# A fused attention and cosine FFN on one core: tile 0 cut in two halves around tile 1, with the start ordered from a list of pieces

## The chip, the cores and the metric

The kernel runs on one core of a Trainium2 chip. The metric is the device time of one execution in microseconds (us). Five engines matter here: TensorE (PE in the profile; its weight loads are listed as PEld), VectorE (DVE), ScalarE (ACT), GpSimd (POOL) and SyncE (SP), which issues the DMAs. Each engine runs its own instructions in a fixed order and waits on semaphores.

## The reference, cut to what matters

```
def reference(q, k, v, w_in, w_out):          # q, k, v: 8 x 8 heads x 576 x 64, float32
    ...                                       # split into 9 chunks of 64 along the sequence
    scores = scale * np.matmul(q_c, k_c.transpose(0, 1, 2, 4, 3))     # 64 x 64 per chunk
    scores = scores - np.max(scores, axis=-1, keepdims=True)
    attn = np.exp(scores)
    attn = attn / (np.sum(attn, axis=-1, keepdims=True) + 1e-09)
    out = np.matmul(attn, v_c)
    x = out.transpose(0, 2, 1, 3).reshape(4608, 512)
    h = x @ w_in                              # 512 x 2048
    g = h * np.cos(h)
    return (g @ w_out).astype(np.float32)     # 2048 x 512
```

The attention is local to chunks of 64 tokens. The two weights come as 8-byte floats; everything else is 4-byte.

## The kernel before, in words

The 4608 tokens are nine tiles (t = 0 to 8) of 512 tokens. d_ff is cut into 16 chunks (fc) of 128. For each tile there is attention, which makes x, and then 16 steps. A step has one `hidden(t, fc)` (L333), which makes h for one chunk of d_ff, one `activate(t, fc, h)` (L347), which makes g = h cos h, and one `project` (L366), which adds g times a chunk of w_out into the four banks acc0 to acc3. Project runs LAG = 3 steps behind hidden.

Precision is kept by splitting each operand of the big products into a high and a low part and multiplying high by high, high by low and low by high: three matmuls in place of one. Hidden is therefore 4 x 3 = 12 matmuls of 128x128 by 512 columns, and project is 12 as well. All of them are recorded on the helper line L74.

*Weights.* `load_weight` (L98) brings each chunk in as 8-byte words, 512 KB for each of w_in and w_out. `split_weight` (L111) makes 4-byte words of them and splits these: on ACT L124, L125 and L126 and the high part at L136; on DVE L127, L130 and the low part at L137. There are 32 such weights (16 w_in, 16 w_out). They are split once, during tile 0, and stay in SBUF for all tiles. The decoded words lie in a buffer `w` with two places and in `half0` and `half1`; later the same buffers carry output to DMA.

*Activation.* ACT makes a whole number of turns from h (L353), DVE subtracts it (L354), ACT takes the sine (L356), DVE multiplies by h (L357), ACT copies the high part (L360) and DVE makes the low part (L361). h lies in one of two PSUM banks, which come free after L357.

*Attention.* `scores_early` (L175) and `scores` (L191) write scores to PSUM; DVE takes the largest of each row and subtracts it; ACT takes the exponential; DVE sums, inverts and multiplies (the quotient); the weights of the values are transposed, on PE for tiles 0 and 1 (`transposed`, L258) and on DVE for later ones (`turned`, L273); `weighted` (L290) multiplies with the values, and ACT and DVE split the result into the high and low parts of x (L321, L322). The score matmuls and those of `weighted` are 64x64; for a later tile they come in four groups of 64 recorded matmuls. In tile 1 the quotient is one instruction on POOL (L232). Exponentials and sines need different tables on ACT, and changing them is a table load.

*What sets the order.* The main loop (L461) runs over s = 16 t + fc, tiles in turn. During tile t the attention of tile t + 1 is done in its steps (`attend`, `attend_early`). From tile 1 on (`ordered`) every PE, ACT and DVE instruction keeps program order, and the pieces of attention stand in three queues (`soon`, `late`, `full`) from which `activate` takes. For tile 0, before that flag is set, the order on each engine is chosen by the framework's own scheduler. `split_weight` is called AHEAD = 2 chunks ahead. DMAs, all on SP, are ordered by that scheduler throughout.

*Buffers.* x of a tile takes four buffers of a pool of eight; two of tile 0's values borrow one of them. The scores `e` of a tile have one buffer. At a tile's last project `finish` (L380) copies each acc bank (two on ACT, L389, two on DVE, L391) and sends it out.

Of the kernel before, what the change touches and what calls it, by code (L numbers as in the profile page):

```python
# [20 lines left out]
P = 128  # L21
# [8 lines left out]
AHEAD = 2  # L30
# [10 lines left out]
def attention_then_cos_ffn(ctx: ExitStack, tc, qT, kT, v, w_in, w_out, out, wide):  # L41
# [24 lines left out]
    ordered = False  # L66

    def kept(ins):
        if ordered:
            tc.keep_in_program_order(ins)  # L70
        return ins
# [39 lines left out]
    def split_weight(name, fc):  # L111

        raw, n = w_raw.pop((name, fc))
        w = dec.tile([P, n], F32, name="w")
        if not wide:
            nc.gpsimd.tensor_copy(w, raw[:, :n])
        else:
            top = raw[:, 4 : 4 + 4 * n].rearrange("p (n k) -> p n k", k=4)[:, :, 0]
            mid = raw.bitcast(U32)[:, 1 : 1 + 2 * n].rearrange("p (n k) -> p n k", k=2)[:, :, 0]


            half, low = half_words[(name == "out")], w.bitcast(U32)
            hb = half[:, :, 1]
            nc.scalar.activation(hb.bitcast(BF16), top.bitcast(BF16), AF.Abs)  # L124
            nc.scalar.activation(hb, hb, AF.Relu, bias=float(7 - (MORE << 7)), scale=8.0)  # L125
            nc.scalar.activation(low, mid, AF.Relu, bias=float((1 << 19) - 1), scale=-(2.0**-13))  # L126
            nc.vector.scalar_tensor_tensor(  # L127
                hb, top, 0x8000, hb, op0=ALU.bitwise_and, op1=ALU.bitwise_or
            )
            nc.vector.tensor_tensor(  # L130
                low, low, half.rearrange("p n k -> p (n k)").bitcast(U32), op=ALU.bitwise_xor
            )
        o = SHIFT if name == "in" else 0
        parts = wts.tile([P, 2 * n + PAD], F32R, name=f"w_{name}{fc}")
        hi, lo = parts[:, o : o + n], parts[:, o + n : o + 2 * n]
        nc.scalar.copy(out=hi, in_=w)  # L136
        nc.vector.tensor_tensor(lo, w, hi.bitcast(F32), op=ALU.subtract)  # L137
        w_parts[name, fc] = (hi, lo)
# [6 lines left out]
    probs = {}  # L145
    def load_qk(t, hp):
        qt, kt = (att.tile([P, TOK], F32, name=n, bufs=HP) for n in ("qt", "kt"))
        nc.sync.dma_start(out=qt, in_=qT[t, hp])
        nc.sync.dma_start(out=kt, in_=kT[t, hp])
        queries[t, hp] = (qt, kt)  # L150

    def load_v(t, hp):

        if t or hp < 2:
            vt = att.tile([P, TOK], F32, name="vt")
        else:
            if hp == 2:
                values["roomy"] = xp.tile([P, 2, TOK], F32, name="x")
            vt = values["roomy"][:, hp - 2]
# [10 lines left out]
    def weights_of(t):  # L170
        if t not in probs:
            probs[t] = att.tile([P, HP, NCH, CH], F32, name="e", bufs=1)
        return probs[t]

    def scores_early(t, hp, s):  # L175

        qt, kt = queries.pop((t, hp))
        for c in range(NCH):
# [5 lines left out]
        e = weights_of(t)  # L184
        m = att.tile([P, NCH], F32, name="m", bufs=4)
        nc.vector.tensor_reduce(out=m, in_=sv, op=ALU.max, axis=AX.X)
        nc.vector.tensor_tensor(
            e[:, hp], sv, m.unsqueeze(2).broadcast_to([P, NCH, CH]), op=ALU.subtract
        )

    def scores(t, g, banks):  # L191
# [14 lines left out]
        e = weights_of(t)[:, 2 * g : 2 * g + 2].rearrange("p a (r h) k -> p a r h k", h=2)  # L206
        for h in range(2):
# [10 lines left out]
            soon.extend((largest, below))  # L218

    def softmax(t, a, b):  # L220

        n = (b - a) * NCH
        e = probs[t][:, a:b].rearrange("p a c k -> p (a c) k")
        nc.scalar.activation(e, e, AF.Exp, scale=SCALE)
        z = att.tile([P, HP * NCH], F32, name="z")
        zs = z[:, :n]
        nc.vector.tensor_reduce(out=zs, in_=e, op=ALU.add, axis=AX.X)
        nc.vector.tensor_scalar(zs, zs, 1e-9, None, op0=ALU.add)
        nc.vector.reciprocal(out=zs, in_=zs)

        eng = nc.gpsimd if t == 1 else nc.vector
        eng.tensor_tensor(e, e, zs.unsqueeze(2).broadcast_to([P, n, CH]), op=ALU.mult)  # L232

    def exponentials(t):
        e = probs[t].rearrange("p a c k -> p (a c k)")
        kept(nc.scalar.activation(e, e, AF.Exp, scale=SCALE))

    def divide(t):

        z = att.tile([P, HP, NCH], F32, name="z")  # L240

        def total(hp):
            kept(nc.vector.tensor_reduce(out=z[:, hp], in_=probs[t][:, hp], op=ALU.add, axis=AX.X))

        def inverse():
            kept(nc.vector.tensor_scalar(z, z, 1e-9, None, op0=ALU.add))
            kept(nc.vector.reciprocal(out=z, in_=z))

        def quotient(hp):
            e = probs[t][:, hp]  # L250
            zb = z[:, hp].unsqueeze(2).broadcast_to([P, NCH, CH])
            kept(nc.vector.tensor_tensor(e, e, zb, op=ALU.mult))

        soon.extend(lambda hp=hp: total(hp) for hp in range(HP))
        soon.append(inverse)
        return [lambda hp=hp: quotient(hp) for hp in range(HP)]

    def transposed(t, hp):  # L258


        e = probs[t][:, hp]
        pts = att.tile([P, TOK], F32, name="pts")
        pt = ps_h.tile([P, 512], F32, name="h") if t == 0 else bank("a", 0)
        for c in range(0, NCH, 2):
            nc.tensor.transpose(
# [3 lines left out]
            )  # L269
        nc.scalar.copy(out=pts, in_=pt)  # L270
        probs[t, hp] = pts

    def turned(t, hp):  # L273
# [3 lines left out]
        src = probs[t][:, hp].rearrange("p c (x k) -> p c x k", k=BL)  # L277
# [12 lines left out]
    def weighted(t, hps, banks):  # L290
# [18 lines left out]
        if (t, g) not in x_parts:  # L309
            x_parts[t, g] = tuple(  # L310
                xp.tile([P, 2, TOK], F32R, name="x") for _ in range(2)
            )
        for par in range(2):
# [6 lines left out]
            def split(xq=xq, hi=hi, lo=lo):  # L320
                kept(nc.scalar.copy(out=hi, in_=xq))  # L321
                kept(nc.vector.tensor_tensor(lo, xq, hi.bitcast(F32), op=ALU.subtract))  # L322

            if t < EARLY:
                split()
            else:
                late.append(split)


    g_parts = {}  # L330
    acc = {}

    def hidden(t, fc):  # L333
        if t == 0 and fc in (2, 3):
            h = bank("a", fc)
        else:
            h = ps_h.tile([P, TOK], F32, name="h")
# [9 lines left out]
    def activate(t, fc, h):  # L347
# [5 lines left out]
        kept(nc.scalar.activation(n, h, AF.Identity, bias=0.25, scale=0.5 / math.pi))  # L353
        kept(nc.vector.scalar_tensor_tensor(g, n, -2.0 * math.pi, h, op0=ALU.mult, op1=ALU.add))  # L354
        take(soon, 1)
        kept(nc.scalar.activation(g, g, AF.Sin, bias=0.5 * math.pi))  # L356
        kept(nc.vector.tensor_tensor(g, h, g, op=ALU.mult))  # L357
        take(soon, 1)
        take(full, 2)
        kept(nc.scalar.copy(out=g_hi, in_=g))  # L360
        kept(nc.vector.tensor_tensor(g_lo, g, g_hi.bitcast(F32), op=ALU.subtract))  # L361
        g_parts[t, fc] = (g_hi, g_lo)
# [3 lines left out]
    def project(t, fc):  # L366
        g_hi, g_lo = g_parts.pop((t, fc))
        w_hi, w_lo = w_parts["out", fc]
        for sub in range(NSUB):
            if fc == 0:  # L370
# [3 lines left out]
            matmul(o, g_hi[:, ss], w_hi, start=(fc == 0), stop=False)  # L374
            matmul(o, g_hi[:, ss], w_lo, start=False, stop=False)
            matmul(o, g_lo[:, ss], w_hi, start=False, stop=(fc == NFC - 1))
            if fc == NFC - 1:
                full.append(lambda sub=sub, o=o: finish(t, sub, o))

    def finish(t, sub, o):  # L380
        if t == NT - 1:
            if sub % 2 == 0:
                acc["last"] = xp.tile([P, 2, DM], F32, name="x")
            os = acc["last"][:, sub % 2]
        else:

            os = (wts if sub % 2 else dec).tile([P, DM], F32, name=f"half{sub // 2}" if sub % 2 else "w")
        if sub % 2 == 0:
# [3 lines left out]
        r0 = t * TOK + sub * P  # L392
        nc.sync.dma_start(out=out[r0 : r0 + P, :], in_=os)


    def attend_early(t, step):
        if step < HP:
            scores_early(t, step, bank("a", step))
        if step == HP - 1:
            softmax(t, 0, HP)  # L400
        hp, odd = divmod(step - HP - 1, 2)
        if 0 <= hp < HP and not odd:
            transposed(t, hp)
            weighted(t, (hp,), (bank("a", 0), bank("a", 1)))
            if hp + 2 < HP:
                load_v(t, hp + 2)
# [3 lines left out]
    def attend(t, step):  # L410

        for g in range(2):
            if step == g:
                scores(t, g, (bank("a", 0), bank("a", 1)))
            if step == 8 + 5 * g:
                weighted(t, (2 * g, 2 * g + 1), (bank("a", 0), bank("a", 1)))
# [3 lines left out]
        if step == 3:  # L420
            pieces["quotients"] = divide(t)

        soon.extend(pieces["quotients"][a] for a in {4: (0, 1), 5: (2,), 6: (3,)}.get(step, ()))
# [12 lines left out]

    for hp in range(HP):
        load_qk(0, hp)
    load_weight("in", 0)
    for hp in range(HP):  # L440
        load_v(0, hp)
    for fc in range(NFC):
        if fc:
            load_weight("in", fc)
# [92 lines left out]
```

## Time and profile before

| | us |
|---|---|
| median of 3 runs (lowest, highest) | 880.68 (880.52, 880.91) |
| the profiled execution | 880.95 |
| its span, first to last instruction | 879.1 |
| PE busy in the span | 853.0 |
| mean granted PE clock | 0.986 |

| stage of the span, us | DMA, GB/s | granted PE clock |
|---|---|---|
| 10 to 20 | 409 | 0.79 |
| 20 to 30 | 401 | 0.50 |
| 30 to 40 | 406 | 0.67 |
| 50 to 60 | 405 | 1.00 |
| 70 to 80 | 0 | 1.00 |
| 200 to 300 | 43 | 1.00 |

A row of the timeline has its start, its duration, the engine, the line, the operation, the tile that it writes and those it reads, the shapes and a count; in brackets is how long the engine was idle before it and what released it. Matmuls are pipelined, so the durations of matmuls that follow each other overlap; the distance of their starts is what one costs. "x" in a count column is a number of instructions. Line numbers are those of the kernel before.

### The profile page before, as it was taken

How to read it: one execution, taken by the hardware profiler on the slowest of the kernel's cores; microseconds unless marked ns; L12 is line 12 of the kernel's file. 1: busy time of each engine (PE TensorE's matmuls, PEld its weight loads, DVE VectorE, ACT ScalarE, POOL GpSimd, SP SyncE). 2: the span in 40 equal slices, each digit the busy share in tenths (PEclk: the TensorE clock that was granted, in tenths of full speed). 3: DMA queues.
4: the chain of work that ended last, by engine and by line, in shares of the span. 5: the costliest groups of instructions: out<-in, count | busy, mean ns of one | idle time of the engine just before them, and what ended most of it. 6: DMA issues, size and time to landing. Idle time of an engine off the chain costs nothing.

```text
span 879.1 us, 14100 instructions
## 1 busy us (share of the span) xinstructions
PE 853.0 (97%) x5792; PEld 697.1 (79%) x5792; DVE 576.7 (66%) x975; ACT 407.9 (46%) x660; POOL 5.5 (1%) x9
## 2 busy tenths in 40 slices
PE   4899999999999999999999999999999999999998
PEld 3587777888888888888888888888888888888886
DVE  5999986766577656764686558655766577644332
ACT  4998993533354335333533344333533354333332
POOL 0001000000000000000000000000000000000000
PEclk8599999999999999999999999999999999999999
DMA  9980013100310012001300040003100010001001
GB/s 346 406 340 33 14 25 110 47 26 25 96 49 25 24 49 96 25 1 50 120 1 25 25 145 1 25 25 97 49 25 25 1 48 25 1 1 48 1 1 48
DMA packets 25407, 55.42 MB, mean 63 GB/s; under 512 B 2816, under 2 KB 2816, under 8 KB 25344
## 3 DMA queue, kind: packets, MB, share of 16 engines
q1 hardware_dynamic: 25344, 54.54, 17.7%
q8 instruction: 45, 0.74, 0.4%
q14 instruction: 18, 0.15, 0.1%
HBM read 45.09 MB, written 9.44 MB: 62 GB/s over the span
## 4 chain that ended last, share of the span: by engine, by line
PE 85%; ACT 11%; DMA 1%; DVE 1%; issue 1%; SPq 0%; ACTq 0%
PE acc L74 41%; PE h L74 40%; PE a L74 4%; ACT half L124 2%; ACT half L125 2%; ACT w L126 2%; DMA w_out<-in_w_out_dram 1%; ACT g_hi L360 1%; ACT g L356 1%; ACT w_out L136 1%; ACT w_in L136 1%; ACT g L353 1%; DMA kt<-in_kT_dram 1%; ACT pts L270 0%; ACT x L321 0%
## 5 line engine op out<-in xcount | busy, mean ns | idle before, releaser
L74 PE MATMUL h<-x,w_in 128*128 128x512 f32 x1704 | 416.9, 393 | 5.9 <-ACT x L321 2.8
L74 PEld LDWEIGHTS h<-x,w_in 128*128 128x128 f32 x1704 | 321.1, 189 | 75.0 <-DVE g L357 4.5
L74 PE MATMUL acc<-w_out,g_hi 128*128 128x512 f32 x1152 | 355.2, 392 | 0.0
L74 PEld LDWEIGHTS acc<-w_out,g_hi 128*128 128x128 f32 x1152 | 214.0, 188 | 45.2
L74 PE MATMUL acc<-w_out,g_lo 128*128 128x512 f32 x576 | 221.1, 390 | 0.6 <-DVE g_lo L361 0.6
L354 DVE SCALAR_TENSOR_TENSOR g<-g,h 128x512 f32<-128x512 int32 x142 | 97.2, 684 | 138.3 <-ACT g L353 137.6
L353 ACT ACTIVATE g<-h 128x512 int32<-128x512 f32 x142 | 84.7, 596 | 190.1 <-PE h L74 190.1
L361 DVE TENSOR_TENSOR g_lo<-g,g_hi 128x512 fp32r<-128x512 f32 x144 | 102.5, 712 | 79.9 <-ACT g_hi L360 77.0
L356 ACT ACTIVATE g<-g 128x512 f32<-128x512 f32 x144 | 91.0, 632 | 128.2 <-DVE g L354 128.0
L360 ACT CAST g_hi<-g 128x512 fp32r<-128x512 f32 x144 | 89.3, 620 | 128.9 <-DVE g L357 79.3
L357 DVE TENSOR_TENSOR g<-h,g 128x512 f32<-128x512 f32 x142 | 98.1, 691 | 56.5 <-ACT g L356 53.0
L74 PEld LDWEIGHTS acc<-w_out,g_lo 128*128 128x128 f32 x576 | 108.1, 188 | 23.7 <-DVE g_lo L361 1.1
L282 DVE STREAM_TRANSPOSE pts<-e 32x256 f32<-32x256 f32 x224 | 97.4, 435 | 3.7
L125 ACT ACTIVATE half<-half 128x512 uint16<-128x512 uint16 x32 | 25.1, 786 | 0.2
L74 PEld LDWEIGHTS a<-kt,qt 64*64 64x64 f32 x1024 | 18.9, 135 | 7.6 <-issue 6.8
L130 DVE TENSOR_TENSOR w<-w,half 128x512 uint32<-128x512 uint32 x32 | 22.0, 687 | 1.8 <-ACT w L126 1.0
L74 PEld LDWEIGHTS a<-pts,vt 64*64 64x64 f32 x1024 | 16.6, 134 | 7.2 <-issue 5.3
L322 DVE TENSOR_TENSOR x<-a,x 128x512 fp32r<-128x512 f32 (+1 forms) x38 | 21.9, 614 | 0.1
L74 PE MATMUL a<-kt,qt 64*64 64x64 f32 x1024 | 21.8, 222 | 0.0
L74 PE MATMUL a<-pts,vt 64*64 64x64 f32 x1024 | 19.0, 222 | 0.7 <-ACT pts L270 0.7
L216 DVE TENSOR_TENSOR e<-a,m 128x512 f32<-128x512 f32 x28 | 19.2, 686 | 0.5
L212 DVE TENSOR_REDUCE m<-a 128x8 f32<-128x512 f32 x28 | 19.2, 684 | 0.0
(61 smaller groups left out, 316.5 us busy)
## 6 DMA issues: line engine op xcount, KB each, us to landing
qt<-in_qT_dram SPq DMA_DIRECT2D x36, 256.0 KB, 4.0
kt<-in_kT_dram SPq DMA_DIRECT2D x36, 256.0 KB, 4.2
vt<-in_v_dram SPq DMA_DIRECT2D x34, 256.0 KB, 3.0
w_in<-in_w_in_dram SPq DMA_DIRECT2D x16, 512.0 KB, 9.1
w_out<-in_w_out_dram SPq DMA_DIRECT2D x16, 512.0 KB, 9.4
out_dram<-w SPq DMA_DIRECT2D x16, 256.0 KB, 2.1
out_dram<-half SPq DMA_DIRECT2D x16, 256.0 KB, 2.0
out_dram<-x SPq DMA_DIRECT2D x4, 256.0 KB, 2.0
```

Of the source, the lines that this page charges most:

```text
L74: kept(nc.tensor.matmul(*args, **kw))
L125: nc.scalar.activation(hb, hb, AF.Relu, bias=float(7 - (MORE << 7)), scale=8.0)
L130: nc.vector.tensor_tensor(low, low, half.rearrange("p n k -> p (n k)").bitcast(U32), op=ALU.bitwise_xor)
L212: kept(nc.vector.tensor_reduce(out=m, in_=sv, op=ALU.max, axis=AX.X))
L282: kept(nc.vector.transpose(out=dst[o : o + BL, :, qb], in_=src[i : i + BL, :, kb]))
L322: kept(nc.vector.tensor_tensor(lo, xq, hi.bitcast(F32), op=ALU.subtract))
L353: kept(nc.scalar.activation(n, h, AF.Identity, bias=0.25, scale=0.5 / math.pi))
L354: kept(nc.vector.scalar_tensor_tensor(g, n, -2.0 * math.pi, h, op0=ALU.mult, op1=ALU.add))
L356: kept(nc.scalar.activation(g, g, AF.Sin, bias=0.5 * math.pi))
L357: kept(nc.vector.tensor_tensor(g, h, g, op=ALU.mult))
L360: kept(nc.scalar.copy(out=g_hi, in_=g))
L361: kept(nc.vector.tensor_tensor(g_lo, g, g_hi.bitcast(F32), op=ALU.subtract))
```

## The change

Tile 0's steps are cut in two: fc 0 to 7 (GROUP = 8) come first, then all 16 steps of tile 1, then fc 8 to 15 of tile 0, then tiles 2 to 8. The sums of tile 0's first half are copied from the acc banks to SBUF, written to a tensor in HBM (`partial`), read back after tile 1's last project (`resume`), and added on DVE when tile 0's second half is done. The second half of the weights is due only from step 16 on.

The instructions of these first 32 steps, with the splitting of all weights and the attention of tiles 0, 1 and 2, are no longer issued as the program comes to them. Each becomes a piece: engine, length, a function that issues it, the pieces that it follows, an earliest time (estimated arrival of a load), and a lag. The pieces get due times backward from the big PE pieces, which are taken to start at WAIT = 23 and to follow each other without a gap; then a list rule picks, for the engine that can start soonest, the piece due earliest among those that can start within 0.2 us of the soonest. The functions are called in that order, and every instruction of PE, ACT, DVE and POOL keeps it (`kept` always holds).

The rest follows from these: in tiles 0 and 1 the exponentials are taken per head pair, and all eight of them before the first sine (`raised`); tile 0's first two quotients and tile 1's four are single POOL instructions of 128x512, where tile 1 had one of 128x2048; tile 1's `weighted` takes two head pairs at a time; `e` is two buffers, e0 and e1; x has two sets of four buffers, x0 for tile 0, x1 for tiles 1 and 2, and then in turn; hidden always uses the two h banks; the loads of tile 1's queries and keys come ahead of the weights, and w_out's two chunks behind w_in's.

The diff, cut to its core:

```
-AHEAD = 2
+GROUP = 8
...
-    xp = ctx.enter_context(tc.tile_pool(name="xp", bufs=8))
+    xp = ctx.enter_context(tc.tile_pool(name="xp", bufs=4))
+    hbm = ctx.enter_context(tc.tile_pool(name="hbm", bufs=1, space=bass.MemoryType.DRAM))
...
     def kept(ins):
-        if ordered:
-            tc.keep_in_program_order(ins)
+        tc.keep_in_program_order(ins)
...
+    def x_room(t, dtype):
+        return xp.tile([P, 2, TOK], dtype, name=f"x{(t + (t > 1)) % 2}")
...
+    order = [(0, fc) for fc in range(GROUP)] + [(1, fc) for fc in range(NFC)]
+    order += [(t, fc) for t in range(NT) if t != 1 for fc in range(0 if t else GROUP, NFC)]
+    partial = [hbm.tile([P, DM], F32, name=f"partial{sub}") for sub in range(NSUB)]
...
+    def finish(t, sub, o, whole):
+        if not whole:
+            os, to = att.tile([P, DM], F32, name="vt" if sub % 2 else "pts"), partial[sub]
+        elif t == 0:
+            os = acc["partial", sub]
...
+        if whole and t == 0:
+            kept(nc.vector.tensor_tensor(os, os, o, op=ALU.add))
...
+    def resume():
+        for sub in range(NSUB):
+            os = acc["partial", sub] = out_room(sub)
+            nc.sync.dma_start(out=os, in_=partial[sub])
...
+    def piece(eng, length, run, *after, at=0.0, lag=0.15):
+        work.append([eng, length, run, [a for a in after if a is not None], at, length + lag])
+        return len(work) - 1
...
+    STAGE = 2 * NFC
+    for fc in range(NFC):
+        s = fc if fc < GROUP else GROUP + fc
+        due["in", fc], due["out", fc] = s, s + LAG
...
+        a = piece(ACT, 0.65, rest_of(key, 0), xored.get(name), at=here[name, fc])
+        r = piece(ACT, 0.65, rest_of(key, 1), a)
+        m = piece(ACT, 0.52, rest_of(key, 2), two_back, at=here[name, fc])
+        g = piece(DVE, 0.63, rest_of(key, 3), r)
+        xored[name] = piece(DVE, 0.6, rest_of(key, 4), m, g)
+        h = piece(ACT, 0.52, rest_of(key, 5), xored[name])
+        split[name, fc] = piece(DVE, 0.6, rest_of(key, 6), h)
...
+                if t or hp < 2:
+                    q[hp] = piece(POOL, 1.0, lambda hp=hp: quotient(t, hp, nc.gpsimd), i)
+                else:
+                    q[hp] = piece(DVE, 0.6, lambda hp=hp: quotient(t, hp), i)
...
+            if t and hp == 1:
+                def values_next():
+                    for j in (2, 3):
+                        load_v(t, j)
+                piece(SP, 0.1, values_next, now)
...
+        stream = piece(
+            PE, 2.72, made_by(key, hidden, t, fc), stream, split["in", fc], bank_at,
+            *x_done[t], *([turned_out[0, 1]] if s < 2 else ()),
+        )
...
+        for i, (eng, length) in enumerate(((DVE, 0.6), (ACT, 0.55), (DVE, 0.6), (ACT, 0.53), (DVE, 0.6)), 1):
+            a = piece(eng, length, rest_of(key, i), a, *([projected.get(s - LAG)] if i == 4 else raised if i == 2 else ()))
...
+    WAIT = 23.0
+    clock = WAIT
+    for i, w in enumerate(work):
+        if w[0] == PE and w[1] > 2:
+            due_at[i] = clock
+            clock += w[1]
+    for i in x_done[2]:
+        due_at[i] = clock - 8.0
+    for i in reversed(range(len(work))):
+        for a in work[i][3]:
+            due_at[a] = min(due_at[a], due_at[i] - work[a][5])
...
+                near = [
+                    (d if e != PE or work[i][1] > 2 else 0.0, start, i)
+                    for start, d, i in c if start <= soonest + 0.2
+                ]
...
+    for start, i in sorted(starts):
+        work[i][2]()
...
-    for s in range(NT * NFC + LAG):
+    for s in range(STAGE, len(order) + LAG):
```

More of the change, by code (lines that the diff above doesn't have):

```diff
@@ L127, in split_weight @@
[L127 to L136, printed above, removed]
@@ L234, in exponentials @@
[L234 to L256, printed above, removed]
+            found.extend((largest, below))
@@ new lines, in scores, with exponentials, total @@
+        return found
+    def exponentials(t, *hps):
+        for e in [weights_of(t, hp // 2)[:, hp % 2] for hp in hps] or [weights_of(t, g) for g in range(2)]:
+            e = e.rearrange("p c k -> p (c k)" if hps else "p a c k -> p (a c k)")
+            kept(nc.scalar.activation(e, e, AF.Exp, scale=SCALE))
+    sums = {}
+    def total(t, hp):
+        if hp == 0:
+            sums[t] = att.tile([P, HP, NCH], F32, name="z")
+        kept(nc.vector.tensor_reduce(out=sums[t][:, hp], in_=weights_of(t, hp // 2)[:, hp % 2], op=ALU.add, axis=AX.X))
@@ L420, in attend @@
         if step == 3:
-            pieces["quotients"] = divide(t)
-        soon.extend(pieces["quotients"][a] for a in {4: (0, 1), 5: (2,), 6: (3,)}.get(step, ()))
+            soon.extend(lambda hp=hp: total(t, hp) for hp in range(HP))
+            soon.append(lambda: inverse(t))
+        for hp in {4: (0, 1), 5: (2,), 6: (3,)}.get(step, ()):
+            soon.append(lambda hp=hp: quotient(t, hp))
         if 4 <= step < 8 or 9 <= step < 13:
@@ new lines, in attention_then_cos_ffn, with made_by, go, rest_of @@
+    made = {}
+    def made_by(key, run, *args):
+        def go():
+            made[key] = run(*args)
+        return go
+    def rest_of(key, i):
+        return lambda: made[key][i]()
+    STAGE = 2 * NFC
+    segment = {x: s for s, x in reversed(list(enumerate(order)))}
+    due = {}
+    for fc in range(NFC):
+        s = fc if fc < GROUP else GROUP + fc
+        due["in", fc], due["out", fc] = s, s + LAG
+    split = {}
+    xored = {}
+    turn_of = sorted(due, key=lambda b: (due[b], b))
@@ new lines, in attention_then_cos_ffn @@
+    WAIT = 23.0
+    clock = WAIT
+    due_at = [1e9] * len(work)
+    for i, w in enumerate(work):
[7 more added lines that the diff above has]
+            due_at[a] = min(due_at[a], due_at[i] - work[a][5])
+    free_at = [0.0] * 5
+    ends = {}
+    starts = []
+    todo = set(range(len(work)))
+    while todo:
+        best = None
+        can = [[] for _ in range(5)]
+        for i in todo:
+            if all(a in ends for a in work[i][3]):
+                e = work[i][0]
+                start = max([free_at[e], work[i][4]] + [ends[a] for a in work[i][3]])
+                can[e].append((start, due_at[i], i))
+        for e, c in enumerate(can):
+            if c:
+                soonest = min(c)[0]
+                near = [
+                    (d if e != PE or work[i][1] > 2 else 0.0, start, i)
+                    for start, d, i in c if start <= soonest + 0.2
+                ]
+                d, start, i = min(near)
+                if best is None or start < best[0]:
+                    best = (start, i)
+        start, i = best
+        todo.remove(i)
+        starts.append((start, i))
+        free_at[work[i][0]] = start + work[i][1]
+        ends[i] = start + work[i][5]
```

411 lines of the change are left out of this document (292 added, 119 removed).

## The prediction

> **What bounds the kernel now.** I read the page's totals first, then busy time by stage, then TensorE (PE) in order of time, then the chain of waits for ScalarE (ACT) and the timeline of VectorE (DVE).
>
> ```profile
> span 879.1 us, 14100 instructions
> PE 853.0 (97%) x5792; PEld 697.1 (79%) x5792; DVE 576.7 (66%) x975; ACT 407.9 (46%) x660; POOL 5.5 (1%) x9
> ```
>
> A share of 97% seems to leave PE nothing to gain. It is a mean, and busy time also counts matmuls that run at a lower clock. The stages say more (columns: stretch, its length, then busy time and instructions of PE, PEld, DVE, ACT, POOL; granted clock, DMA share, GB/s; the borders are explained below):
>
> ```profile
> 6.35:20.00 13.65, 6.75 (x136) 6.04 (x136) 11.55 (x22) 7.36 (x13) 0.00 (x0) 0.85 1.03 398
> 20.00:69.49 49.49, 43.47 (x364) 33.42 (x357) 45.74 (x81) 49.14 (x89) 0.00 (x0) 0.80 0.93 362
> 69.49:140.70 71.21, 65.90 (x461) 51.50 (x460) 62.76 (x98) 62.16 (x111) 3.89 (x1) 1.00 0.09 25
> ```
>
> From 20 to 69.49 us ACT is busy 49.14 of 49.49 us and DVE 45.74: the weights are decoded and split there, beside tile 0's steps. To see what PE has to show for it I count in units: a unit is 12 matmuls of 512 columns, one hidden or one project. Matmuls that read w_in, then those that read w_out, in the first 69.49 us and after 140.70 us; then two steps of the last tile, and a step with a group of 64 attention matmuls:
>
> ```profile
> 0.00:69.49 69.49, 22.39 (x72) 0.83 0.93 356
> 0.00:69.49 69.49, 11.33 (x48) 0.83 0.93 356
> 140.70:879.10 738.40, 366.02 (x1524) 1.00 0.12 39
> 140.70:879.10 738.40, 378.15 (x1561) 1.00 0.12 39
> ...
> 780.20 2.88 PE L74 MATMUL h<-x,w_in 128*128 128x512 f32 x12
> 785.64 2.88 PE L74 MATMUL h<-x,w_in 128*128 128x512 f32 x12
> ...
> 226.28 2.88 PE L74 MATMUL h<-x,w_in 128*128 128x512 f32 x12
> 229.10 1.16 PE L74 MATMUL a<-kt,qt 64*64 64x64 f32 x64
> 233.04 2.88 PE L74 MATMUL h<-x,w_in 128*128 128x512 f32 x12
> ...
> 875.18 0.39 PE L74 MATMUL acc<-w_out,g_lo 128*128 128x512 f32 x1
> ```
>
> A step (two units) takes 785.64 - 780.20 = 5.44 us, so a unit takes 2.72. A step with an attention group takes 233.04 - 226.28 = 6.76, so the group costs 1.32. After 140.70 us there are (1524 + 1561)/12 = 257 units and 27 groups (four for each of tiles 2 to 8, one of them done): 140.7 + 257 x 2.72 (699.0) + 27 x 1.32 (35.6) = 875.3, and the last matmul ends at 875.57. So nothing is lost after 140.7; there the kernel is PE at full rate. All loss lies before. By 69.49 us PE has done (72 + 48)/12 = 10 units, worth 27.2 us; from there to 140.70 it does 21 units, 57.1 us of work in 71.2, beside tile 1's attention. The change touches this start and must be judged there.
>
> **The yardstick.** Call T8 the time at which tile 1's first hidden (step 8 of the new order) can start. Before it PE must have done 8 hidden and 5 projects: 13 units. Attention of tile 1, w_in 0 to 7 and w_out 0 to 4 must be done: 13 weights. Afterwards 275 units (748.0) and 28 groups (37.0) are left, then the tail of 879.1 - 875.57 = 3.5, and the profiled execution's own time of 880.95 is 1.85 above its span. It lies 0.27 above the median 880.68, which I neglect.
>
> **ACT up to T8.** Pieces of its chain of waits (start, length to the next piece, what), and one with the table load:
>
> ```profile
> 91.87 0.51 ACT w_in L136
> 92.38 0.69 ACT half L124
> 93.07 0.42 ACT pts L270
> 93.49 0.56 ACT w L126
> 94.05 0.68 ACT half L125
> 94.73 0.46 ACT g_hi L360
> 95.19 0.49 ACT g L353
> 97.47 0.47 ACT g L356
> 99.77 0.21 ACT x L321
> ...
> 79.12 1.28 ACT L356
> ```
>
> A weight is 0.51 + 0.69 + 0.56 + 0.68 = 2.44; 13 of them 31.7. A step's activation is 0.49 + 0.47 + 0.46 = 1.42; five whole ones and two without the last copy (which their banks don't need) are 9.0. Eight exponentials at 0.47, taken like the sine of that size, 3.8; eight copies of transposes at 0.42, 3.4; x copies of tile 0 eight at 0.21 and of tile 1 four at 0.46, 3.5; one table load 1.3. Sum 52.7.
>
> ```profile
> 6.35 0.69 DVE L186 TENSOR_REDUCE m<-acc 128x8 f32<-128x512 f32 x1 [6.35 <-PE acc L74]
> 7.80 0.63 ACT L224 ACTIVATE e<-e 128x512 f32<-128x512 f32 x1 [5.79 <-DVE e L187]
> ```
>
> ACT starts at 7.80 and loses 12.2 - 7.36 = 4.8 by 20 us waiting for data, and 0.35 after; the loads at the front don't get faster. 7.8 + 52.7 + 5.2 = 65.7.
>
> **DVE up to T8.** Starts of instructions that follow each other:
>
> ```profile
> 61.05 0.70 DVE L357 TENSOR_TENSOR g<-a,g 128x512 f32<-128x512 f32 x1
> 61.65 0.70 DVE L130 TENSOR_TENSOR w<-w,half 128x512 uint32<-128x512 uint32 x1
> ...
> 63.66 0.75 DVE L127 SCALAR_TENSOR_TENSOR half<-w_out,half 128x512 uint16<-128x512 uint16 x1
> 64.31 0.67 DVE L361 TENSOR_TENSOR g_lo<-g,g_hi 128x512 fp32r<-128x512 f32 x1
> ```
>
> 0.60 for a 512-wide one, 0.65 for L127. A weight 1.85, 13 of them 24.1; activations 5 x 1.8 + 2 x 1.2 = 11.4; tile 0 twelve (largest, below, total) 7.2, two quotients 1.2, inverses 0.7, eight half-size x parts about 3 (an estimate: half of 0.60 and a little); tile 1 the same without quotients and with four full x parts, 10.3. Sum 57.9. It starts at 6.35 and idles 2.1 to 20 us and 3.75 after: 6.35 + 57.9 + 5.85 = 70.1.
>
> Six quotients (two of tile 0, four of tile 1) go to POOL. In the kernel before the one POOL quotient shows what that does:
>
> ```profile
> 82.81 3.89 POOL L232 TENSOR_TENSOR e<-e,z 128x2048 f32<-128x2048 f32 x1 [80.63 <-ACT w L126]
> 83.14 0.68 DVE L354 SCALAR_TENSOR_TENSOR g<-g,h 128x512 f32<-128x512 int32 x1
> 83.73 3.52 DVE L361 TENSOR_TENSOR g_lo<-g,g_hi 128x512 fp32r<-128x512 f32 x1
> ```
>
> While POOL works, a DVE operation that reads PSUM (h) runs on in 0.68, and one with two SBUF operands takes 3.52 instead of about 0.7. A quarter of 3.89 is 0.97, so six hold DVE for 0 to 5.8 us. I take 2: some of what stands in line reads PSUM. That makes DVE 72. The Trainium skill, GPSIMD Engine Reference, section Key points, says that GpSimd shares its SBUF interfaces with VectorE and contends with VectorE instructions that have two SBUF inputs; by that alone, with every piece held, T8 would be 76 and the whole 4 us longer. The row agrees.
>
> **PE up to T8.** Tile 0's attention needs its 12.1 of DVE, and beside it stand w_in 0's three and tile 1's first ones (about 2); with the 2.1 idle PE's first hidden starts at 6.35 + 12.1 + 2 + 2 = 22.5. Then 13 units, 35.4, and tile 1's attention, the matmuls into its banks taking 5.96 us from 60 to 129 us. Below that row stand one with which the first hidden was held up, and one at a low clock:
>
> ```profile
> 60.00:129.00 69.00, 5.96 (x172) 1.00 0.12 37
> ...
> 36.88 0.80 PE L74 MATMUL h<-x,w_in 128*128 128x512 f32 x1 [2.02 <-ACT x L321]
> 39.78 4.57 PE L74 MATMUL h<-x,w_in 128*128 128x512 f32 x12
> ```
>
> Say 7 with the first scores: 65. The last row is a unit at a low clock (the stretch 20 to 69.49 has 0.80 in the mean); it takes 4.57 against 2.88 later. Were the first three cold, +5: 70. So three engines end between 65 and 76, and I take **T8 = 72**, DVE's value.
>
> **After T8.** ACT and DVE owe w_out 5 to 7 over three steps: DVE 5.6 + 5.4 of activations in 16.3 us of PE. Weights 8 to 15 come due from step 16 on, and steps 8 to 15 leave DVE 43.5 - 14.4 us for them; tile 2's attention falls under steps 16 to 31 (87 us; about 27 of DVE). All is covered, if the order on each engine, now fixed, fits the real times. Edits that I cost at nothing: the four copies of half sums at step 10 (ACT, DVE, 0.6 each) lie beside hidden of step 11, 2.72; uncovered, 1.2. Four DMAs out and four back, issued by SP behind loads that nothing waits for then: eight steps stand between reading back and use; the half sums are 16 steps old. Tile 0's final sums are four DVE additions instead of two copies on each engine, +1.2 of DVE where it is busy two thirds. Tile 2's x takes tile 1's room, free after step 23 and due at 32; misplaced, its copy on ACT would hold the next sine for at most a step, 5.4. For all stalls of the fixed order I take 1.5, bounds 0 and 10 (the slowest landing of values, below).
>
> **Sum:** 72 + 748.0 + 37.0 + 3.5 + 1.85 + 1.5 = 863.9, so **864 us**, 17 less. A second way to it: before, 69.49 + 278 x 2.72 + 37 + 3.5 + 1.85 would be 868.0, and 880.95 is 12.9 more, lost between 69.5 and 140.7 to tile 1's attention and to waits. After, 3 units more (8.2) stand at a time 2.5 later, and 1.5 of the 12.9 comes back: -5.7 - 11.4 = -17.
>
> **Rivals.**
> *Values late.* The second half of tile 1's values is asked for only after its first weighted sum, while the weights still stream, and the plan allows no time for its landing:
>
> ```profile
> DMA to landing us min/median/max: 2.5/6.2/9.5
> ```
>
> PE, now in fixed order, could stand at the second weighted sum for 9.5 less the 3 that the steps between take: 6.5, so 870. For: the queues are busy 0.93 of the stretch from 20 to 69.49 us. Against: PE has other work due ahead. It stays faster.
>
> *The gain doesn't arrive.* The list rule places work so that 10 units are done when 10 were: then 878 to 882. Against: for that ACT and DVE would have to be idle a good part of the time, and the list starts whatever is ready.
>
> *Slower: a cold PE.* Up to T8 PE waits in every step, and its clock could stay at half: 13 units then cost 70.8, T8 = 22.5 + 70.8 + 7 = 100, the whole 892. It decides from T8 = 90.5 on (882.4), when more than 9 of the 13 units run cold. For: 0.80 in the mean up to 69.49, and 4.57 for a unit. Against: from 69.49 on PE idles 5.3 of 71.2 and keeps 1.00, and a cold PE is busy all the time. The Trainium skill, TensorE: Matmul & The Clock Gate, Part 1, has the gate open after about 3.4 us of sustained work; by that the cold time ends by itself after one or two units, which the clock of 1.00 after 69.49 bears out.
>
> *Better than 855:* ACT's bound of 65.7 holds for all and nothing stalls: 856, so only a little is below.
>
> **How the numbers follow.** Forecast (T8 64 to 78, stalls 0 to 4: 855 to 872) 0.70; values late or the like (866 to 876) 0.13; better 0.04; no gain 0.04; cold PE or a fixed order that loses as much 0.09. The bound of 0.2% is 1.8 us, so the same is 878.9 to 882.4. Faster 0.87, same 0.04, slower 0.09. The range 855 to 874 holds the forecast and most of the late values, 0.80.
>
> **What would show it.** In the profile after: 13 units done when tile 1's first hidden starts, at 72 (64 to 78), as against 10 at 69.5; first hidden at 23 to 26, where before it was still held up at 36.88; two-input DVE instructions stretched to about 1 us beside six POOL ones; from T8 on a step every 5.44 us plus 1.32 for a group, with no PE idle above 2 us; HBM written 1 MB more. Wrong would be: PE at under 0.6 of its clock past 40 us, T8 beyond 80, or PE idle after T8 that adds to over 5 us.

## The result and the profile after

The changed kernel takes 875.70 us (four runs, 874.99 to 876.39) against 880.69: a ratio of 0.9943, 95% interval 0.9926 to 0.9960. It is faster, but by 5.0 us, not by 17, and it lies above the forecast range of 855 to 874. In runs 5, 13 and 16 below one execution of four took 2.2 to 3.0 ms; all times here are medians of the other, fast executions, and no row of runs 5 and 13 is shown, whose profiles are of such an execution. The profiled execution took 875.92, its span is 873.9. The totals of its page:

```profile
span 873.9 us, 14147 instructions
PE 852.0 (97%) x5792; PEld 697.3 (80%) x5792; DVE 576.2 (66%) x974; ACT 408.8 (47%) x664; POOL 8.7 (1%) x14
HBM read 46.14 MB, written 10.49 MB: 65 GB/s over the span
```

The half sums are there (1.05 MB more written, and as much read), and so are the POOL quotients (five instructions more). The same stage as before, 20 to 69.49 us, and one part of it, then matmuls that read w_in and w_out up to 69.49:

```profile
20.00:69.49 49.49, 42.20 (x332) 33.24 (x332) 41.72 (x70) 41.60 (x73) 3.82 (x4) 0.89 0.93 364
28.00:37.00 9.00, 5.60 (x61) 4.79 (x58) 4.85 (x9) 3.34 (x7) 0.00 (x0) 0.65 1.03 405
...
0.00:69.49 69.49, 24.08 (x84) 0.88 0.93 356
0.00:69.49 69.49, 11.93 (x48) 0.88 0.93 356
```

ACT was busy 49.14 of these 49.49 us before the change; now it is 41.60, and DVE went from 45.74 to 41.72. PE has done (84 + 48)/12 = 11 units at 69.49 us where it had done 10; the forecast had 13 by 72. Most of what ACT lost is in the second row: from 28 to 37 us it works 3.34 of 9 us, DVE 4.85, at a PE clock of 0.65. Line numbers from here on are those of the kernel run: L375 in the change, L377 where the loads are pinned, is the product of h with its sine, after which the h bank is free. PE's timeline, up to tile 1's first hidden, shows where (project rows left out):

```profile
24.57 2.99 PE L73 MATMUL h<-x,w_in 128*128 128x512 f32 x12
27.49 1.15 PE L73 MATMUL a<-kt,qt 64*64 64x64 f32 x32
32.04 1.97 PE L73 MATMUL a<-kt,qt 64*64 64x64 f32 x32 [3.40 <-DMA kt<-in_kT_dram]
33.95 4.68 PE L73 MATMUL h<-x,w_in 128*128 128x512 f32 x12
40.80 7.30 PE L73 MATMUL h<-x,w_in 128*128 128x512 f32 x24 [2.17 <-DVE g L375]
...
79.17 1.64 PE L73 MATMUL h<-x,w_in 128*128 128x512 f32 x6
82.05 0.50 PE L73 MATMUL h<-x,w_in 128*128 128x512 f32 x1 [1.24 <-ACT x L335]
82.89 1.44 PE L73 MATMUL h<-x,w_in 128*128 128x512 f32 x5 [0.34 <-DVE x L338]
84.16 0.62 PE L73 MATMUL acc<-w_out,g_hi 128*128 128x512 f32 x2
```

The last four rows give T8: tile 1's first hidden ends at 84.16, less its 2.72 is **81.4**, against 72. The first hidden comes at 24.57, near the forecast. But the scores of tile 1's last pairs wait for keys until 32.04, the second hidden stands behind them, and the third starts only at 40.80. Why it does is in the other engines' timelines (first DVE and ACT instruction after the wait; then the first sine):

```profile
34.05 0.69 DVE L211 TENSOR_REDUCE m<-a 128x8 f32<-128x512 f32 x1 [4.04 <-PE a L73]
35.99 1.23 ACT L254 ACTIVATE e<-e 128x512 f32<-128x512 f32 x2 [5.66 <-DVE e L215]
38.00 1.28 ACT L374 ACT_TABLE_LOAD   x1
39.30 0.63 ACT L374 ACTIVATE g<-g 128x512 f32<-128x512 f32 x1
```

Scores, largest, exponentials, table load, first sine, and only then the third hidden, which needs that step's h bank. In this run the keys start that chain; run 1 below shows how much of it stays without them. The SP queue (start, duration, line, what is loaded) says why they are late:

```profile
11.67 0.33 SPq L170 DMA_DIRECT2D qt<-in_qT_dram  x1
12.27 0.33 SPq L171 DMA_DIRECT2D kt<-in_kT_dram  x1
14.52 0.33 SPq L104 DMA_DIRECT2D w_out<-in_w_out_dram  x1
...
17.66 0.33 SPq L170 DMA_DIRECT2D qt<-in_qT_dram  x1
18.91 0.33 SPq L171 DMA_DIRECT2D kt<-in_kT_dram  x1
...
22.84 0.33 SPq L170 DMA_DIRECT2D qt<-in_qT_dram  x1
24.08 0.33 SPq L171 DMA_DIRECT2D kt<-in_kT_dram  x1
```

The kernel lists tile 1's four pairs of queries and keys ahead of all weights but the first, and its piece list reckons with their arrival at 14 to 18 us. But DMAs aren't pinned: the scheduler set two pairs behind weights. The last was issued at 24.08 and used at 32.04.

The sum again, with T8 as measured: 81.44 + 748.0 + 37.0 + 3.5 = 869.9, and the span is 873.9, so 4.0 us were lost after T8, where 1.5 was forecast. Of the 12.0 us that the profiled execution is above the forecast, 9.4 are T8's and 2.5 these.

### The profile page after: what moved, and what is told of

Read it like the earlier page. It is cut to its first block, busy times and chain, and to the rows that moved or that the text cites. A ratio compares the mean times of both kernels' runs of the same rounds, so it can differ in the third digit from the quotient of the medians.

```text
span 873.9 us, 14147 instructions
## 1 busy us (share of the span) xinstructions
PE 852.0 (97%) x5792; PEld 697.3 (80%) x5792; DVE 576.2 (66%) x974; ACT 408.8 (47%) x664; POOL 8.7 (1%) x14
## 4 chain that ended last, share of the span: by engine, by line
PE 84%; ACT 7%; DVE 4%; DMA 4%; issue 1%; SPq 0%; DVEq 0%
PE acc L73 41%; PE h L73 39%; PE a L73 4%; DMA kt<-in_kT_dram 1%; ACT half L134 1%; ACT half L135 1%; DVE half L138 1%; DMA w_out<-in_w_out_dram 1%; DVE w L141 1%; ACT w L136 1%; DMA qt<-in_qT_dram 1%; ACT w_out L148 1%; ACT g L374 1%; ACT g_hi L376 1%; ACT w_in L148 0%
## 5 line engine op out<-in xcount | busy, mean ns | idle before, releaser
L73 PEld LDWEIGHTS h<-x,w_in 128*128 128x128 f32 x1728 | 325.6, 189 | 75.3 <-ACT w_in L148 3.4
L73 PE MATMUL acc<-w_out,g_hi 128*128 128x512 f32 x1152 | 359.4, 393 | 0.1
L73 PE MATMUL acc<-w_out,g_lo 128*128 128x512 f32 x576 | 224.7, 390 | 0.0
L377 DVE TENSOR_TENSOR g_lo<-g,g_hi 128x512 fp32r<-128x512 f32 x144 | 99.4, 691 | 73.8 <-ACT g_hi L376 70.6
L375 DVE TENSOR_TENSOR g<-h,g 128x512 f32<-128x512 f32 x144 | 99.5, 691 | 55.5 <-ACT g L374 52.4
L254 ACT ACTIVATE e<-e 128x1024 f32<-128x1024 f32 (+1 forms) x22 | 19.0, 899 | 14.6 <-DVE e L215 14.5
L261 DVE TENSOR_REDUCE z<-e 128x8 f32<-128x512 f32 x36 | 23.9, 678 | 1.3 <-ACT e L254 1.3
L271 DVE TENSOR_TENSOR e<-e,z 128x512 f32<-128x512 f32 x30 | 20.3, 683 | 0.1
```

What stands on the lines that cost most here:

```text
L73: kept(nc.tensor.matmul(*args, **kw))
L261: kept(nc.vector.tensor_reduce(out=sums[t][:, hp], in_=weights_of(t, hp // 2)[:, hp % 2], op=ALU.add, axis=AX.X))
L375: lambda: kept(nc.vector.tensor_tensor(g, h, g, op=ALU.mult)),
L377: lambda: kept(nc.vector.tensor_tensor(g_lo, g, g_hi.bitcast(F32), op=ALU.subtract)),
```

## The experiments

All times are medians, as said; the kernel before ran beside each at 880.7 to 881.3. "List" is the kernel's piece list; where an edit changes the pieces or their lengths, the list is made anew, and the order of all engines with it. The runs stand in the order in which they were made.

**1. The loads in the listed order.** Three places in the loaders; the list is untouched.

```
-            nc.sync.dma_start(out=raw[:, 1 : 1 + 4 * n], in_=src.bitcast(U16))
+            kept(nc.sync.dma_start(out=raw[:, 1 : 1 + 4 * n], in_=src.bitcast(U16)))
...                                  # load_qk for t < 2, load_v for tile 0 and tile 1's first two: the same
```

> The first loads (both tiles' queries and keys, tile 0's values, all weights) are pinned on SP in the order in which the kernel lists them, which is the order that its piece list reckons with; nothing else changes. Theory A (the third and fourth pair of tile 1's queries and keys stand behind weights on SP and land at 32 us instead of 18; with the order of every engine fixed, PE stops 3.4, DVE 4.0 and ACT 5.7 us there): no stop between 28 and 37 us, T8 at 75 to 76 instead of 81.4, the whole 869 to 871. Rival B (ACT and DVE have as much to do before T8 in any case, the gap only moves): 874 to 877, ACT idle as much at another place.

**871.78** (871.36 to 871.92), ratio 0.990 (0.9884 to 0.9917): 3.9 us better than the change as it came, and the intervals don't meet. The same rows of PE, and the window in which the gap was:

```profile
28.00:37.00 9.00, 4.97 (x65) 4.03 (x62) 7.33 (x13) 7.46 (x13) 0.00 (x0) 0.89 1.03 409
...
29.43 3.07 PE L73 MATMUL h<-x,w_in 128*128 128x512 f32 x12
36.53 8.21 PE L73 MATMUL h<-x,w_in 128*128 128x512 f32 x24 [4.03 <-DVE g L377]
...
75.09 1.64 PE L73 MATMUL h<-x,w_in 128*128 128x512 f32 x6
78.02 0.50 PE L73 MATMUL h<-x,w_in 128*128 128x512 f32 x1 [1.29 <-ACT x L337]
78.85 2.06 PE L73 MATMUL h<-x,w_in 128*128 128x512 f32 x5 [0.34 <-DVE x L340]
80.70 1.06 PE L73 MATMUL acc<-w_out,g_hi 128*128 128x512 f32 x2
```

ACT works 7.46 of the 9 us instead of 3.34, and the second hidden comes at 29.43, no longer held by keys. The third still waits, 4.0 us for the first sine's result, and starts at 36.53. T8 is 80.70 - 2.72 = 78.0: 3.5 earlier, the gain within 0.5 us. Theory A fits better than rival B (874 to 877), but it promised more: T8 at 75 to 76, 869 to 871 us, and no stop between 28 and 37 us, where PE stands idle from 32.5 on.

**2. The sines free of the exponentials.**

```
-            a = piece(..., *([projected.get(s - LAG)] if i == 4 else raised if i == 2 else ()))
+            a = piece(..., *([projected.get(s - LAG)] if i == 4 else ()))
```

> The sines no longer wait in the list for all eight exponentials of tiles 0 and 1; the loads stay as they are. Rival C (it is the barrier in front of the first sine that costs): ACT's gap at 30 to 36 us closes and the whole gains 3 us or more, 872 or less. Theory A: PE and DVE stop for the keys in any case, since their orders still have the scores in front; the gain is under 2 us, or a loss of 1 to 4 where exponentials and sines now alternate and each change is a table load of 1.28 us.

**877.38**, 1.7 worse than the change. Eight table loads stand where there were two (the first 90 us, ACT):

```profile
L254 ACT ACT_TABLE_LOAD x4 | 5.1, 1283 | 0.8 <-PEq L824 0.7
L374 ACT ACT_TABLE_LOAD x4 | 5.1, 1283 | 0.1
```

Without the barrier nothing is gained, as theory A had it, and six more table loads of 1.28 us are paid. The list was made anew too, so the 1.7 us needn't be theirs alone.

**3. The list told when the keys land.**

```
+    here["qk", 1, 2], here["qk", 1, 3] = 26.5, 31.5
```

> The list is told when tile 1's third and fourth pair really land (26.5 and 31.5 us, where it reckoned with about 16.6 and 17.9); SP's order is left to the scheduler. Theory A: ACT and DVE do weights in the time in which they now stand still, so most of their 5.7 and 4.0 us comes back, though the first sine still waits for the last exponential: 870 to 873. Rival B: 874 to 877.

**873.89** (872.45 to 875.44; 0.991 to 0.994): above theory A's range and just below rival B's. It is 1.8 better than the change, about half of what pinning gave, but the intervals meet, so it isn't shown that a list that knows of a late load loses less to it.

**4. The quotients on DVE.**

```
-                    q[hp] = piece(POOL, 1.0, lambda hp=hp: quotient(t, hp, nc.gpsimd), i)
+                    q[hp] = piece(DVE, 0.6, lambda hp=hp: quotient(t, hp), i)
```

> All eight quotients of tiles 0 and 1 on DVE, none on POOL. The prediction took 2 us of DVE lost to POOL's six quotients; the trace shows about 1.6 (L153 1.30 and L138 1.59 instead of 0.69 and 0.75, L141 0.84). Against that stand six quotients of 0.60 more on DVE, 3.6. So if DVE is what ends last before T8: 1 to 2 us slower, 876 to 878. If POOL's hold costs what the upper bound had, 5.8: 2 us faster, 873 to 874. If neither engine is the bound: within 1 us.

**875.48**, no difference. Either six DVE instructions more are worth about what POOL's six cost, or neither engine is the bound; this run doesn't tell which.

**5. Tile 0 whole.** As run 1, with GROUP = 16; tile 0's output goes out directly, and x of the tiles takes x0 and x1 in turn.

> Loads pinned as in the run with loads pinned (871.8 us), the piece list kept, but tile 0 whole ahead of tile 1 (GROUP = 16, no half sums; x of the tiles in turn). It tells what the two halves bring by themselves. Theory H (ACT is the bound of the start, so asking for half the weights later is what pays): before tile 1's first hidden ACT owes 29 weights, 70.8, activations 20.6 and attention 12, so tile 1 starts at 120 or later with 29 units done, and ACT's delay shows in PE: 4 to 10 us slower than with halves, 876 to 882. Rival P (PE is the bound from 36 us on, where it is busy 22.7 of 23 us): within 2 us of 871.8.

**876.73**, ratio 0.9952 (0.9936 to 0.9969): 5.0 slower than with halves. So with the list and ordered loads alone the kernel gains some 4 us on the kernel before, and the two halves, with the order that the list makes of them, bring the other 5. Rival P falls. The time lies in theory H's range; that ACT is the reason isn't shown by it, and runs 13 and 14 speak against it.

**6. Loads ordered, sines free.** The edits of 1 and 2 together.

> Loads pinned, and the sines don't wait in the list for all eight exponentials (two edits tried one by one before: 871.8 and 877.4 us). The first hidden that waits for the first sine started at 36.5 us with loads pinned, 4.0 us of it PE's wait. Theory S (the first sine behind tile 1's exponentials sets when PE runs without a gap): it starts near 33, but three more pairs of table loads (1.28 each, 7.7 us of ACT) take that back: 871 to 876. If the table loads cost nothing because ACT isn't the bound: 868.

**878.75**, 7.0 slower than run 1: worse than either guess.

**7 and 8. Tile 1's exponentials in one burst**, after the sine of step 3, and of step 1; on top of run 1.

```
+            first = raised[:HP] if s <= BURST else raised
+            if i == 2 and s == BURST:
+                for j in raised[HP:]:
+                    work[j][3].append(a)
```

> Loads pinned; only tile 0's four exponentials come before the first sine, and tile 1's four together after the sine of step 3, so the tables change twice more instead of six times. Theory S: third hidden at 31 instead of 36.5 us, no PE wait of 4.0 us, T8 3 to 6 us earlier less what two table loads take: 866 to 869. Rival P2 (ACT and DVE have no room, the wait only moves to a later step): 871 to 873.

> As the run with the burst after the sine of step 3, but after the sine of step 1. Theory S: the third hidden as early (31 us), so also 866 to 870; the fifth, which waits for the sine of step 2, stands behind the burst, some 1 to 2 us worse than after step 3.

**879.62** and **879.21**: 7 to 8 us slower than run 1, outside both guesses. PE in the first of these two, and behind it the first rows of run 1:

```profile
24.64 3.42 PE L73 MATMUL a<-kt,qt 64*64 64x64 f32 x64 [4.31 <-DVE x L340]
27.99 5.83 PE L73 MATMUL h<-x,w_in 128*128 128x512 f32 x24
35.57 5.99 PE L73 MATMUL h<-x,w_in 128*128 128x512 f32 x24 [0.67 <-DVE g L377]
60.57 4.57 PE L73 MATMUL h<-x,w_in 128*128 128x512 f32 x12 [4.07 <-DVE g L377]
82.91 1.45 PE L73 MATMUL h<-x,w_in 128*128 128x512 f32 x5 [0.84 <-DVE x L340]
```

```profile
22.45 2.08 PE L73 MATMUL a<-kt,qt 64*64 64x64 f32 x64 [2.44 <-DVE x L340]
24.46 3.02 PE L73 MATMUL h<-x,w_in 128*128 128x512 f32 x12
```

The third hidden's own wait did fall, from 4.03 to 0.67 us. But it starts at 35.57, only 1.0 earlier than in run 1, since the scores ahead of the first hidden now wait 4.31 us for DVE instead of 2.44, and the first hidden comes 3.5 later. What was gained by then is lost again: the hidden of step 6 waits 4.07 us for the product of step 4, whose bank it takes, and runs at the low clock behind that (granted 0.50 from 62.5 to 65 us), and tile 1's first hidden is where it was without ordered loads (its last five at 82.91, against 82.89). Theory S falls: in this order the wait for the first sine was moved to other places, not removed.

**9 and 10. Less work for ACT, or for DVE.** On top of run 1, one instruction of each weight's decoding becomes `nothing`, and its piece gets length 0.

> Loads pinned (871.8 us), and each weight's second ACT instruction (the shift of the exponent, L135) is left out, in the list too; the decoded weights are wrong by that. It takes about 0.68 us of ACT from each of 32 weights, 14 of which are split before tile 1 starts: 9.5 us. Theory W (the start is bound by the sum of what ACT has to do, and the bursts were slow because they added table loads to it): T8 6 to 9 us earlier, 863 to 866. Rival V (DVE is as full, 93% busy from 6 to 79 us): 868 to 870. Rival P (PE alone): 871 to 872.

> Loads pinned, and each weight's first DVE instruction (the sign, L138) is left out, in the list too; the decoded weights are wrong by that. It takes about 0.65 us of DVE from each weight, 9 us before tile 1 starts. Theory W (ACT): the chain of a weight is shorter but ACT's sum is the same, so 0 to 2 us: 870 to 872. Rival V (DVE is the bound): 864 to 867.

Less ACT: **878.18**, 6.4 *slower*. Less DVE: **869.28**, 2.5 faster. (The 93% above is 90: in run 1 DVE is busy 65.6 of the 73 us from 6 to 79.) Theory W, that ACT's sum is the bound, has no room for the first. It could be the order, which the list makes from the lengths; runs 13 and 14 test that.

**11 and 12. A shorter first part.** As run 1, GROUP = 6 and GROUP = 4.

> Loads pinned, and tile 0's first part has 6 steps instead of 8 (GROUP = 6); all else as in the run with 871.8 us. By theory W what counts is how much ACT owes before tile 1 can start: four weights less, two activations less, 12 us of ACT for four units, 10.9 us of PE. Before step 6 ACT owes 9 weights (22) and 4.5 activations (6.4); with attention 12, a table load, some work ahead of its time (4) and 13 of start and idle that is 59, and 279 units, 37 and 5.4 from there are 860, with 4 of stalls 864. PE's way, from the third hidden at 36.5 on, ends at 62 and gives 867. So 864 to 868. If the size of the first part doesn't matter: 871 to 873.

> As before with GROUP = 4. Tile 1's attention is then due after four steps, and from step 8 to 19 every step needs two new weights: ACT 4.9 + 1.4 = 6.3 us a step against PE's 5.44, so up to 10 us are lost in tile 1. Theory W: slower than with 6, 868 to 878. If only the first start counts: 862 to 866.

**878.97** and **890.27**. The largest waits of PE (engine, line, waited for; sum, times, longest), first for 6, then for 4:

```profile
PE a L73 <- DMA vt<-in_v_dram: 7.8, 1, 7.8
```

```profile
PE a L73 <- DMA vt<-in_v_dram: 17.0, 1, 17.0
```

This is the prediction's rival "values late", but not for the reason given there, a slow landing. It didn't come with 8 steps; with 6 and 4 the second half of tile 1's values is needed earlier, and stands on SP behind tile 2's queries and keys.

**13 and 14. The same work left out, the order unchanged.** As runs 9 and 10 with DVE (13) and ACT (14), but the piece keeps its length in the list.

> Loads pinned (871.8 us); each weight's first DVE instruction (L138) is left out, but its piece keeps its length in the list, so all other instructions keep their order; the decoded weights are wrong by that. About 0.65 us of DVE less per weight, 9 us before tile 1 starts. If DVE is the bound of the start, as the forecast had it: T8 4 to 8 us earlier, 864 to 868. If ACT is, 870 to 872. If the fixed order and its waits are, whichever engine is relieved: 868 to 870 in this and in the run with less ACT.

> Loads pinned; each weight's second ACT instruction (L135) is left out, its piece keeps its length in the list, so the order of all other instructions stays; the decoded weights are wrong by that. About 0.66 us of ACT less per weight. If ACT is the bound of the start: 864 to 867. If DVE is: 870 to 872. If the list order is what made the earlier run without L135 slow (878.2): clearly under 878 here.

**868.03** and **868.10**, both 3.7 faster than run 1. Run 14 and the run with less ACT at 878.18 leave out the same 32 instructions; the list's order alone is 10.1 us between them (for DVE, runs 10 and 13, it is 1.2, within the noise). And relief of either engine helps alike and little (some 9 us taken off, under 4 gained), as the third guess of the first expectation had it: if one engine alone were the bound, relief of the other would give 870 to 872. No single engine bounds this start. Stages of run 14 (37 to 60, 60 to 81.44, 81.44 to 140.70 us):

```profile
37.00:60.00 23.00, 22.55 (x92) 18.21 (x92) 22.48 (x37) 18.24 (x33) 2.49 (x2) 0.88 1.03 406
60.00:81.44 21.44, 20.55 (x206) 15.61 (x207) 20.92 (x34) 19.83 (x37) 2.50 (x2) 1.00 0.30 103
81.44:140.70 59.26, 59.26 (x379) 48.68 (x378) 57.10 (x92) 48.76 (x83) 0.00 (x0) 1.00 0.18 63
```

With ACT at 18.24 of 23 us, PE and DVE are full all the same. What it gains on run 1 is mostly won by tile 1's second hidden, which comes 2.5 us earlier (81.98 against 84.46): T8 is 79.24 - 2.72 = 76.5 instead of 78.0, and no low clock follows it (1.00 in the second row, where run 1 has 0.95). Its rows:

```profile
79.24 0.62 PE L73 MATMUL acc<-w_out,g_hi 128*128 128x512 f32 x2
81.98 2.96 PE L73 MATMUL h<-x,w_in 128*128 128x512 f32 x12
```

**15. No POOL quotients**, the list unchanged.

```
+                    q[hp] = piece(POOL, 1.0, lambda: None, i)
```

> Loads pinned; POOL's six quotients are left out (the attention of tile 1 and of half of tile 0 isn't normalised), the list is unchanged. It prices POOL: its hold on DVE (stretched instructions of 0.6 to 0.9 us, about 1.6 in sum by the trace) and its time in the chain of tile 0 (PE waits 2.6 us for the first two quotients). If only the hold counts: 870 to 871. If the chain of tile 0 counts too: 867 to 870. If neither: 871 to 872.

**870.71**, 1.1 faster, with intervals that meet. So the whole price of POOL in this kernel, hold and chain together, is about 1 us and not clear of the noise.

**16. Six steps with the values in time.** As the run with 6, tile 1's values and then tile 2's queries and keys pinned too.

> GROUP = 6 with loads pinned (879.0 us), and also tile 1's second half of values pinned ahead of tile 2's queries and keys on SP, which were issued 52 to 61 us, before them. If the 7.8 us that PE waited for these values are what made 6 slower than 8: 870 to 873. If the size 6 by itself costs: 876 to 879. If a shorter first part pays, as theory W had it: 864 to 868.

**872.73**, 6.2 faster than 878.97: the late values were most of what 6 lost. Against 871.78 with 8 steps, a shorter first part brings nothing.

## Why the prediction was wrong

*What bounds the kernel, and where.* Right in the main: little is lost late, and nearly all of the difference arises before T8 and in the steps up to 140.87 us. The sum from T8 on (748.0 + 37.0 + 3.5) holds within 4.0 us.

*"The loads at the front don't get faster" (ACT up to T8).* This is the step that failed first, and with it T8 = 72, which measured 81.4. It took over the idle time of before, 5.2 us for ACT and 5.85 for DVE. But the change puts tile 1's scores into the fixed order of PE at a place where their keys, in the scheduler's order of SP, aren't there: 3.4 us of PE, 4.0 of DVE and 5.7 of ACT in one gap. I had read that DMAs are ordered by the scheduler throughout, and not drawn the conclusion. Putting the order right gave back 3.9 us, 3.5 of them before T8.

*PE up to T8.* It had 13 units follow each other from 22.5 on. There are two h banks, so the third hidden needs the first sine, and that stands behind all eight exponentials and a table load. The list shows this wait (`raised`), and I had no term for it. In run 1, without late keys, it is still 4.0 us, and by 36.5 only two units are done. From 36.5 on PE is nearly full: to 78.0 it does 11 units (29.9), tile 1's transposes and weighted sums (about 4) and loses 2.4 to the clock. By these terms 65 should have been near 73. Of the other 5 us to 78.0, 2.9 are in tile 1's first hidden itself, which waits 1.29 and 0.34 us for tile 1's x and then runs slowly (80.70 - 75.09 = 5.61 us instead of 2.72); the rest is short waits and longer units.

*DVE, T8 = 72.* This is the term that the sum went by. From 6.35 us to T8 DVE was idle 11.0 us, where the forecast had 5.85, and busy 64.1, where it had 57.9 and 2 for POOL's hold: 5.2 and 4.2 of the 9.4 us. Part of the busy time was for later steps (15 weights begun and 14 finished, where 13 were due). With the loads in order (run 1) the idle time is 7.1 and the busy time 64.5. But these sums don't make DVE the bound by itself (runs 13 and 14). Taking the largest of three sums was the wrong rule here: three engines with sums so near each other, tied by a fixed order, end later than the largest of them. Runs 9 and 14 show how much the order can make: with the same instructions they lie 10 us apart.

*POOL's hold, 2 us.* Not contradicted: 1.1 with all that hangs on it, not clear of the noise (run 15). The bound of 5.8 was far off.

*Stalls after T8, 1.5.* Too small: 4.0. About half is one step, in which PE waits for DVE in tile 2's scores; from hidden to hidden it takes 8.73 us instead of 6.76:

```profile
132.14 2.88 PE L73 MATMUL h<-x,w_in 128*128 128x512 f32 x12
...
135.09 0.29 PE L73 MATMUL a<-kt,qt 64*64 64x64 f32 x2
136.93 1.16 PE L73 MATMUL a<-kt,qt 64*64 64x64 f32 x62 [1.55 <-DVE e L245]
...
140.87 2.88 PE L73 MATMUL h<-x,w_in 128*128 128x512 f32 x12
```

*Edits costed at nothing.* No wait of PE's matmuls in the change is for half sums, their DMAs or the four additions; one of its weight loads waits 0.4 us for a copy of them, and the step with the copies takes 5.74 us instead of 5.44. x of tile 2 held nothing. That is read from the trace and not tried by itself.

*The rivals.* The change as it came doesn't meet late values: they are issued at 70.49 us, and no row of PE's waits names them. That 875.70 lies in that rival's 866 to 876 is luck in part, since the load that came late was another, tile 1's keys. "The gain doesn't arrive" (878 to 882) didn't come either: 11 units are done where 10 were. The cold PE came as a part, not as the whole: 1.8 and 1.5 us in two places (4.68 and 7.30, against 2.9 and 5.8), not for 9 units. The two halves did what they are for (5.0 us, run 5).

*The signs.* The first hidden (24.57), the 1 MB more written and the stretched DVE instructions (1.30 and 1.59 us beside POOL) came, these longer than the 1 us said. T8 beyond 80 was named as a sign of being wrong, and it came.

What stays open: why one order is up to 10 us better than another of the same pieces. Runs 9 and 14 show that it is the order; which of its many waits decides was not separated. And as the list was made anew in runs 2 to 12 and 16, what their edits cost by themselves isn't separated from what the new order costs.

## What to carry to other kernels

If a list orders the engines, let it order the queue of loads as well, or check in the trace that each load lands when the list thinks: a late load in front of a fixed order stops every engine behind it. When several engines' sums come out close together (here 65 to 72), don't forecast the largest; look for the chain that ties them (here two banks, a barrier and a table load), and add its waits. And after each edit of such a list read the whole start again, for an edit that only takes work away can make it slower.

## What the runs showed of the hardware

Not expected: how short a wait is enough for the lower clock, and that its length alone doesn't tell. The prediction had PE keep 1.00 through 5.3 us of idle in 71. Here a unit that follows a wait takes 2.9 to 3.1 us, or is stretched. Rows of five kernels (waits of 4.07 and 0.67 in run 7 stand above): run 10, with less work for DVE; run 6, loads ordered and sines free; run 9, with less work for ACT; run 8, a burst after step 1; run 3, the list told:

```profile
34.75 3.05 PE L73 MATMUL h<-x,w_in 128*128 128x512 f32 x12 [2.34 <-DVE g L375]
```

```profile
40.30 4.59 PE L73 MATMUL h<-x,w_in 128*128 128x512 f32 x12 [2.50 <-DVE g L377]
```

```profile
36.56 3.08 PE L73 MATMUL h<-x,w_in 128*128 128x512 f32 x12 [2.70 <-DVE g L377]
```

```profile
48.58 4.60 PE L73 MATMUL h<-x,w_in 128*128 128x512 f32 x12 [3.23 <-DVE g L377]
```

```profile
38.49 5.49 PE L73 MATMUL h<-x,w_in 128*128 128x512 f32 x12 [5.62 <-DVE g L375]
```

After 0.67, 2.34 and 2.70 us nothing is lost (granted clock 1.00 from 35 to 40 us in runs 9 and 10); after 2.50, 3.23 and 4.07 about 1.6, after 4.03 in run 1 2.4 (two units in 8.21 instead of 5.83), after 5.62 some 2.5. In the change 2.17 us cost 1.5 (7.30 for two units; granted clock 0.69 from 40 to 42.5 us), shortly after an earlier low stretch (0.50 from 32.5 to 37.5 us). And the two short waits at the end of run 1's start, 1.29 and 0.34, were followed by 2.06 us for five matmuls, where the change, after 1.24 and 0.34, took 1.44. What decides between them isn't shown. The Trainium skill, TensorE: Matmul & The Clock Gate, Part 1, has the gate close after an idle window of about 3.4 us whose borders run freely. The rows agree that idle time brings the lower clock, but 2.17 and 2.50 us of waiting were already enough here.
